# A recurrent-memory attention kernel: the software-DMA ring in SBUF is cut from 16 KB to 4 KB, and three more weight pieces stay resident

## The chip, the core and the metric

The kernel runs on one core of one Trainium2 chip. The metric is the device time of one execution in microseconds (us); lower is better. A core has TensorE (PE; its weight loads are shown as PEld), VectorE (DVE), ScalarE (ACT), GpSimd (POOL) and SyncE (SP), a memory SBUF of 128 partitions, an accumulator memory PSUM of eight banks, and 16 DMA engines that move data between HBM and SBUF. Here SyncE issues the loads of weights, ScalarE and GpSimd issue the other transfers. GpSimd's DMAs are described by software: a piece of each SBUF partition is set aside as a ring in which their descriptors are written.

## The reference

```python
# A: attention with a recurrent memory. x is 2048 x 1024, 32 heads of 128, mem 8 rows, segments of 32 rows
for s in range(64):
    h = concat([mem, x[32 * s:32 * s + 32]])             # 40 rows
    q, k, v = h @ Wq, h @ Wk, h @ Wv                     # 1024 -> 32 heads x 128
    scores = (q @ k.T) * 128 ** -0.5, masked
    o = softmax(scores) @ v
    o = o @ Wo                                           # 4096 -> 1024
    mem = o[:8]                                          # the memory of the next segment
    outs.append(o[8:])
# B: a feed-forward block on the same x, inner width 3584
b = (gelu(x @ w_gate) * (x @ w_up)) @ w_down
g = sigmoid((x * gate_w).sum(-1))
return g * a + (1 - g) * b
```

Each step needs the memory that the step before has made, so the 64 steps run one after the other, and each uses all four weights, 8 MB apiece in bf16.

## The kernel before, in words

The kernel has a prologue (it transposes x, works out the gate, fills the weight slots), a scan of 64 steps, a stage that multiplies the late rows of all segments with Wo (L868), and the feed-forward block with the final mix (from L909 on).

**Pieces and slots.** Each weight is cut into 16 pieces of 128 x 2048 bf16, 512 KB, which is 4 KB of each partition: eight pieces `i` for each half `u` of the heads, 64 pieces `(m, u, i)` with `m` one of k, q, v, o. SBUF holds 50 slots `sl` of that size. A piece is either resident in a slot of its own, or it is one of a pair that shares a slot: `(m, 0, i)` and `(m, 1, i)`, which are loaded in turn. The table `PAIRS` says which `i` are paired, for each weight:

```python
PAIRS = {"k": (1, 3, 5), "q": (0, 2, 5), "v": (0, 2, 4, 6), "o": (0, 2, 4, 6)}
def seq(m, r):
    p = [i for i in range(8) if i in PAIRS[m]]
    f = [i for i in range(8) if i not in p]
    return p + f if r == 0 else f + p
ORDER = (("k", 0), ("q", 0), ("v", 0), ("k", 1), ("q", 1), ("o", 0), ("v", 1), ("o", 1))
```

A step walks through `ORDER` (`r` is the first or second pass over that weight; which half of the heads that is alternates from step to step). In the first pass the paired pieces come first, in the second they come last. As soon as the last use of a paired piece in a step has run on PE (`spent`), the other half is asked for into the same slot (`fetch`, L351, on SyncE's queue); the piece that stays from the second pass is the one that the next step's first pass starts with. So each pair is loaded once per step, 14 loads or 7.3 MB.

**A step on the engines.** `proj` runs the pieces: four matmuls per piece for k, q, v (L662, into the banks X and Y) and eight for o (L674). After each of k, q, v ScalarE copies the bank to `tok` or `vA` (`evac`, L561), PE transposes it (`trans`, L578) and VectorE writes kT or qT. `scores` (L597 to L622) is the score matmul and the softmax, which ends in VectorE's tA and tB; `attend` (L632, L637) multiplies them with vA and vB. Both run twice per step: the scores after the first v and the attention within the second q pass (piece 5), then the scores again after the first o pass and the attention at the start of the second o pass. The step ends in the second o pass, the copy `a_bf`, the transposes at L836 and VectorE's write of the memory rows into hT (L839).

**Work between.** Rows of a segment that don't depend on the memory are projected ahead, four segments at a time: `fill` puts matmuls (L689) into the gaps, `fill_evac` and `fill_put` bring the result through the staging areas kS, qS, oS to the HBM scratch qk_scr and v_scr. From there `load_qk` (L442), `load_v` (L446) and `load_h` (L433) bring in what a step needs. All of these, the store of the result (`store`, L846) and of the late rows (L817) are issued by GpSimd. oS lies on vA's memory, so the copy into vA waits until the stores from oS have landed.

**The end of the scan.** In the last step SyncE's queue gets, after the pieces, the o pieces that the stage L868 needs and that have no slot of their own (`load_xo`, L555), the late rows `oR` (L550), and the first feed-forward weights (L513, L520).

All engines run what the code records in the order of recording; waits are put in from the memory ranges and banks that instructions touch. The sequence on each queue is thus that of the code.

Of the kernel before, what the change touches and what calls it, by code (L numbers as in the profile page):

```python
# [195 lines left out]
def bass_gated_mix__memory_aug_recurrent_mem_tr__geglu_ffn__prompt_kernel(  # L196
# [34 lines left out]
    with ExitStack() as es:  # L231
# [18 lines left out]
        PB = [es.enter_context(nc.psum_tensor(f"pb{i}", [128, 512], FP32)) for i in range(8)]  # L250
        PBV = [p[:, :].bitcast(BF16) for p in PB]

        base = (nc.sbuf_base + 63) // 64 * 64
        top = nc.sbuf_usable_end
        cur = [base]

        def al(name, shape, dt=BF16, at=None):
            if at is None:
                cur[0] = (cur[0] + 63) // 64 * 64
                t = _T(nc, name, shape, dt, cur[0])  # L260
                cur[0] += t.nb
                return t
            return _T(nc, name, shape, dt, at)
# [25 lines left out]
        PIECE = 4096  # L289
        cur[0] = (cur[0] + 63) // 64 * 64  # L290
        res0 = cur[0]
        NSLOT = (top - cur[0]) // PIECE


        PAIRS = {"k": (1, 3, 5), "q": (0, 2, 5), "v": (0, 2, 4, 6), "o": (0, 2, 4, 6)}

        def seq(m, r):
            p = [i for i in range(8) if i in PAIRS[m]]
            f = [i for i in range(8) if i not in p]
            return p + f if r == 0 else f + p  # L300
# [3 lines left out]
        def at_step(p, s):  # L304
            m, r, i = walk[p]
            return (m, r ^ (s % 2), i)

        hosts = []
        for m in "kqvo":
            for i in range(8):  # L310
                if i in PAIRS[m]:
                    hosts.append([(m, 0, i), (m, 1, i)])
                else:
                    hosts += [[(m, 0, i)], [(m, 1, i)]]
        assert len(hosts) <= NSLOT, (len(hosts), NSLOT)
        slots = [al(f"sl{n}", [128, 2048]) for n in range(len(hosts))]
        home = {p: n for n, h in enumerate(hosts) for p in h}
        paired = lambda p: len(hosts[home[p]]) > 1
        uses = [[] for _ in hosts]
        for s_ in range(NSEG):  # L320
            for p in range(64):
                k = at_step(p, s_)
# [49 lines left out]
        for g in range(4):  # L372
            q = slice(32 * g, 32 * g + 32)
# [169 lines left out]
        oR = [al(f"oR{b}", [128, RB, 32], at=tail - (b + 1) * SB * 512) for b in range(NBK)]  # L543
        lost = [("o", 1, i) for i in PAIRS["o"]]
        assert NSEG % 2 == 0
# [185 lines left out]
        for s in range(NSEG):  # L731
            last = s == NSEG - 1
            at = {}
# [258 lines left out]
```

## Time and profile before

| what | value |
|---|---|
| median of 3 runs | 2507.78 us (2507.7, 2507.78, 2512.19) |
| span of the profiled execution | 2512.9 us, 0.7 us above the slowest of the three runs; no other time of that execution is listed |
| busy of the span | PE 84%, DVE 36%, ACT 23%, POOL 23% |
| DMA | 642.77 MB, mean 256 GB/s |
| weight pieces loaded (sl) | 946: Wv 268, Wo 268, Wk 205, Wq 205 |

In lines of the profile the first words are line, engine, operation, tile written and tiles read, with buffer numbers left out. Behind a group's "x" stand the count, then busy us, mean ns, and the idle time before it with what ended it. "SPq" is SyncE's queue of DMA issues. A wait `A <- B: total, times, longest` says that A sat idle until B ended.

### The profile page before, as it was taken

What the parts mean: (1) busy time and instruction counts of PE and PEld (TensorE: products, weight loads), DVE (VectorE), ACT (ScalarE), POOL (GpSimd) and SP (SyncE); (2) the same over time, 40 slices, a digit from 0 to 9 for tenths busy, and PEclk for the clock granted to TensorE, in tenths of its full rate; (3) what the DMA queues carried; (4) which work ended last, traced back from release to release, by engine and by line L of the source; (5) the groups of instructions that cost most, each with busy time, mean ns of one, the idle gap of its engine ahead of it and who ended that gap; (6) DMA issues with size and microseconds to landing.
All of it is one profiled execution on the core that took longest, in us unless ns stands there. A gap on an engine that the chain in (4) does not pass through costs nothing.

```text
span 2512.9 us, 76509 instructions
## 1 busy us (share of the span) xinstructions
PE 2119.3 (84%) x34822; PEld 1062.0 (42%) x34822; DVE 899.3 (36%) x2119; ACT 572.5 (23%) x1175; POOL 587.1 (23%) x1139
## 2 busy tenths in 40 slices
PE   2588888888888888888888888787779999999998
PEld 1244444444444444444444444344445444444443
DVE  3233333333333333333333333333313526354452
ACT  1122222222222222222222222222202303122130
POOL 5223323322332333323333332332200000000000
PEclk9799999999999999999999999999989999999999
DMA  9877887888788788788788788788794070612506
GB/s 359 323 267 280 300 308 281 290 296 296 281 302 309 275 304 317 271 298 317 280 304 305 282 304 310 280 306 313 274 351 175 19 262 5 217 68 91 194 1 218
DMA packets 251859, 642.77 MB, mean 256 GB/s; under 512 B 30344, under 2 KB 43528, under 8 KB 251536
## 3 DMA queue, kind: packets, MB, share of 16 engines
q1 hardware_dynamic: 218128, 584.14, 64.4%
q0 software_dynamic: 23040, 38.87, 5.1%
q10 hardware_dynamic: 10368, 14.88, 1.7%
q8 instruction: 273, 4.47, 0.7%
q14 instruction: 50, 0.41, 0.0%
HBM read 606.29 MB, written 31.39 MB: 254 GB/s over the span
## 4 chain that ended last, share of the span: by engine, by line
PE 44%; DMA 42%; DVE 5%; issue 3%; ACT 3%; POOL 2%; SPq 0%; ACTq 0%; POOLq 0%
DMA sl<-in_A_Wq_dram 17%; DMA sl<-in_A_Wo_dram 14%; PE pb L909 13%; PE pb L674 7%; PE pb L662 7%; PE pb L946 6%; PE pb L689 4%; DMA vB<-v_scr 3%; DMA qk_scr<-oS 3%; PE pb L868 2%; PE pb L578 2%; DMA wd<-in_B_w_down_dram 2%; DMA xr_scr<-xr 1%; ACT tok L561 1%; POOL gp L428 1%
## 5 line engine op out<-in xcount | busy, mean ns | idle before, releaser
L662 PE MATMUL pb<-sl,hT 128*32 128x512 bf16 x12288 | 794.3, 386 | 76.6 <-DMA sl<-in_A_Wq_dram 35.1
L662 PEld LDWEIGHTS pb<-sl,hT 128*32 128x32 bf16 x12288 | 322.2, 97 | 394.5 <-DMA sl<-in_A_Wq_dram 52.3
L674 PE MATMUL pb<-sl,oT 128*32 128x256 bf16 x8192 | 307.1, 292 | 51.1 <-DMA sl<-in_A_Wo_dram 43.6
L561 ACT ACTIVATE tok<-pb 128x512 bf16<-128x512 f32 x320 | 191.3, 598 | 370.3 <-PE pb L662 316.4
L674 PEld LDWEIGHTS pb<-sl,oT 128*32 128x32 bf16 x8192 | 210.8, 103 | 132.8 <-DMA sl<-in_A_Wo_dram 61.9
L689 PE MATMUL pb<-sl,hR 128*32 128x512 bf16 x3072 | 226.8, 393 | 7.4 <-issue 4.0
L909 PE MATMUL pb<-xT,wg 128*128 128x512 bf16 x896 | 211.8, 379 | 8.4 <-DVE GT L925 8.4
L909 PE MATMUL pb<-xT,wu 128*128 128x512 bf16 x896 | 211.7, 379 | 0.0
L646 POOL COPY oRc<-oT 128x128 bf16<-128x128 bf16 x128 | 96.4, 753 | 456.8 <-DVE oT L564 456.8
L946 PE MATMUL pb<-wd,GT 128*128 128x512 bf16 x896 | 195.7, 379 | 3.3 <-DMA wd<-in_B_w_down_dram 3.1
L632 PE MATMUL pb<-tA,vA 32*128 32x40 bf16 x2048 | 36.7, 179 | 143.3 <-DVE tB L622 92.3
L564 DVE COPY qT<-pb 128x512 bf16<-128x512 bf16 x128 | 54.4, 425 | 253.7 <-PE pb L578 240.4
L561 ACT ACTIVATE vA<-pb 128x512 bf16<-128x512 f32 x128 | 76.4, 597 | 279.2 <-DMA v_scr<-oS 106.5
L917 ACT ACTIVATE s<-pb 128x512 f32<-128x512 f32 x112 | 66.8, 596 | 319.2 <-PE pb L909 299.8
L909 PEld LDWEIGHTS pb<-xT,wg 128*128 128x128 bf16 x896 | 86.9, 98 | 116.4 <-DVE GT L925 12.8
L564 DVE COPY kT<-pb 128x512 bf16<-128x512 bf16 x128 | 54.4, 425 | 224.9 <-POOL kT L723 107.9
L946 PEld LDWEIGHTS pb<-wd,GT 128*128 128x128 bf16 x896 | 86.8, 98 | 111.5 <-DMA wd<-in_B_w_down_dram 8.8
L909 PEld LDWEIGHTS pb<-xT,wu 128*128 128x128 bf16 x896 | 87.7, 98 | 105.7
L918 DVE SCALAR_TENSOR_TENSOR tp<-s,pb 128x512 f32<-128x512 f32 x112 | 77.0, 687 | 131.9 <-ACT s L917 131.8
L607 DVE TENSOR_REDUCE st<-pb 128x8 f32<-128x320 f32 x128 | 63.0, 492 | 170.2 <-PE pb L602 170.2
L609 ACT ACTIVATE E<-pb 128x320 bf16<-128x320 f32 x128 | 55.7, 435 | 257.8 <-DVE pb L608 257.5
L561 ACT ACTIVATE oT<-pb 128x160 bf16<-128x160 f32 x256 | 63.8, 302 | 219.5 <-PE pb L637 219.5
(79 smaller groups left out, 1954.7 us busy)
## 6 DMA issues: line engine op xcount, KB each, us to landing
sl<-in_A_Wv_dram SPq DMA_DIRECT2D x268, 512.0 KB, 11.6
sl<-in_A_Wo_dram SPq DMA_DIRECT2D x268, 512.0 KB, 7.3
sl<-in_A_Wk_dram SPq DMA_DIRECT2D x205, 512.0 KB, 5.9
sl<-in_A_Wq_dram SPq DMA_DIRECT2D x205, 512.0 KB, 9.4
wd<-in_B_w_down_dram SPq DMA_DIRECT2D x56, 1024.0 KB, 5.7
qkr<-qk_scr POOLq DMA_DIRECT2D x128, 64.0 KB, 5.8
wg<-in_B_w_gate_dram SPq DMA_DIRECT2D x3, 1792.0 KB, 16.1
wu<-in_B_w_up_dram SPq DMA_DIRECT2D x3, 1792.0 KB, 13.7
```

What stands on the lines that cost most here:

```text
L561: op("act", lambda e: e.activation(o, i, ACTF.Copy), rd=rd, wr=wr)
L564: op("dve", lambda e: e.tensor_copy(o, i), rd=rd, wr=wr)
L607: op("dve", lambda e: e.tensor_reduce(nm, sS, AX.X, ALU.max, negate=True), rd=[BK(SS)], wr=[st8.r(0, 8)])
L609: op("act", lambda e: e.activation(E8[:, :, :].rearrange("p a c -> p (a c)"), PB[SS][:, 0:320], ACTF.Exp, scale=scale), rd=[BK(SS)], wr=[E ...
L646: op("pool", lambda e: e.tensor_copy(oRc[:, :, 16 * u:16 * u + 16].rearrange("p c x -> p x c"), oT[:, :, :, 32:40].rearrange("p g j c -> p ...
L662: ins = e.matmul(PB[bk][32 * g:32 * g + 32, :], lhsT=h[:, i, :], rhs=w[:, g * 512:(g + 1) * 512], start=(p % 8 == 0), stop=(p % 8 == 7))
L674: ins = e.matmul(PB[XO][32 * g:32 * g + 32, 0:256], lhsT=oT[:, gp_, 2 * jj + hh, 0:32], rhs=w[:, c:c + 256], start=(r == 0 and p % 8 == 0 ...
L689: ins = e.matmul(PB[b][32 * g:32 * g + 32, :], lhsT=h[:, k[2], :], rhs=w[:, g * 512:(g + 1) * 512], start=(n == 0), stop=(n == 7))
L909: ins = e.matmul(PB[bk][:, 0:FB], lhsT=w[:, kc, cc:cc + 128], rhs=xT[:, :, :, kc, :].rearrange("p t i c -> p (t i) c"), start=(kc == 0), s ...
L917: op("act", lambda e, hg=hg: e.activation(s1[:, :], hg, ACTF.Square, scale=SQ), rd=[BK(bg)], wr=[s1.r()])
L918: op("dve", lambda e, hg=hg, t=t: e.scalar_tensor_tensor(out=t[:, :], in0=s1[:, :], scalar=1.0, in1=hg, op0=ALU.add, op1=ALU.mult), rd=[BK ...
L946: ins = e.matmul(PB[bank[2 * k + hf]][:, :], lhsT=GT[:, j, tb * 128:(tb + 1) * 128], rhs=w[:, jj, hf * 512:(hf + 1) * 512], start=(j == 0) ...
```

## The change

The ring of descriptors takes 4 KB of each partition instead of 16 KB. The 12 KB behind it are three more slots: the first three of the list lie there (`NLOW`), the others follow where they lay before, so that there are 53. `PAIRS` loses q's 5 and o's 4 and 6, which thereby have slots of their own in both halves. The number of pieces loaded per step falls from 14 to 11 (k 3, q 2, v 4, o 2). What is computed stays the same.

```diff
+        RING = 4096
+        hole = nc.dynamic_dma_scratch_size
+        nc.dynamic_dma_scratch_size = RING
+        for mls in nc.m.functions[0].allocations:
+            if mls.name.startswith("DynamicDMAScratchLoc"):
+                mls.tensor_shape = [128, RING]
+                mls.memorylocations[0].dims = [128, RING]
...
-        NSLOT = (top - cur[0]) // PIECE
-        PAIRS = {"k": (1, 3, 5), "q": (0, 2, 5), "v": (0, 2, 4, 6), "o": (0, 2, 4, 6)}
+        NLOW = (hole - RING) // PIECE
+        NSLOT = NLOW + (top - cur[0]) // PIECE
+        PAIRS = {"k": (1, 3, 5), "q": (0, 2), "v": (0, 2, 4, 6), "o": (0, 2)}
...
-        slots = [al(f"sl{n}", [128, 2048]) for n in range(len(hosts))]
+        slots = [al(f"sl{n}", [128, 2048], at=RING + n * PIECE if n < NLOW else None) for n in range(len(hosts))]
```

Lines of the kernel behind the new ones count nine more (L351 becomes L360). On SyncE's queue, the loads of one step from the first q piece to the last o piece stood like this (the slot's number is the first one in its name):

```order
L351 DMA sl13_85<-in_A_Wq_dram 128x2048
L351 DMA sl16_88<-in_A_Wq_dram 128x2048
L351 DMA sl21_93<-in_A_Wq_dram 128x2048
L351 DMA sl26_98<-in_A_Wv_dram 128x2048
L351 DMA sl29_101<-in_A_Wv_dram 128x2048
L351 DMA sl32_104<-in_A_Wv_dram 128x2048
L351 DMA sl35_107<-in_A_Wv_dram 128x2048
L351 DMA sl38_110<-in_A_Wo_dram 128x2x1024
L351 DMA sl41_113<-in_A_Wo_dram 128x2x1024
L351 DMA sl44_116<-in_A_Wo_dram 128x2x1024
L351 DMA sl47_119<-in_A_Wo_dram 128x2x1024
```

and now stand like this:

```order
L360 DMA sl13_85<-in_A_Wq_dram 128x2048
L360 DMA sl16_88<-in_A_Wq_dram 128x2048
L360 DMA sl27_99<-in_A_Wv_dram 128x2048
L360 DMA sl30_102<-in_A_Wv_dram 128x2048
L360 DMA sl33_105<-in_A_Wv_dram 128x2048
L360 DMA sl36_108<-in_A_Wv_dram 128x2048
L360 DMA sl39_111<-in_A_Wo_dram 128x2x1024
L360 DMA sl42_114<-in_A_Wo_dram 128x2x1024
```

One q load and two o loads are gone; each v load stands one place nearer to the front. On PE, the second o pass of that step, with the transposes of a fill (L713) in it, was this:

```order
L674 MATMUL pb2<-sl39_111,oT_60 32x256 x8
L674 MATMUL pb2<-sl42_114,oT_60 32x256 x8
L674 MATMUL pb2<-sl45_117,oT_60 32x256 x8
L674 MATMUL pb2<-sl48_120,oT_60 32x256 x8
L674 MATMUL pb2<-sl38_110,oT_60 32x256 x8
L713 MATMUL pb3<-ident_49,tok_61 128x128 x4
L674 MATMUL pb2<-sl41_113,oT_60 32x256 x8
L674 MATMUL pb2<-sl44_116,oT_60 32x256 x8
L674 MATMUL pb2<-sl47_119,oT_60 32x256 x8
```

and is now this:

```order
L683 MATMUL pb2<-sl40_112,oT_60 32x256 x8
L683 MATMUL pb2<-sl43_115,oT_60 32x256 x8
L683 MATMUL pb2<-sl45_117,oT_60 32x256 x8
L683 MATMUL pb2<-sl47_119,oT_60 32x256 x8
L683 MATMUL pb2<-sl49_121,oT_60 32x256 x8
L722 MATMUL pb3<-ident_49,tok_61 128x128 x4
L683 MATMUL pb2<-sl51_123,oT_60 32x256 x8
L683 MATMUL pb2<-sl39_111,oT_60 32x256 x8
L683 MATMUL pb2<-sl42_114,oT_60 32x256 x8
```

The count of matmuls is the same. The pieces that come from the stream (sl38, sl41, sl44, sl47 before, sl39 and sl42 now) stand at the end of the pass, two of them now in its last two places.

## The prediction

> **What bounds the kernel now.** I read the page's head first, then the busy time by stage, then who TensorE (PE) waits for in the long middle stage, then single steps in order of time. The head, the stages (columns: window, its length, busy time with instruction counts of PE, PEld, DVE, ACT, POOL, granted clock, share of the 16 DMA engines, GB/s), and the two transposes that close each step (duration in ns, first and last start):
>
> ```profile
> span 2512.9 us, 76509 instructions
> 0.00:112.00 112.00, 40.25 (x469) 22.11 (x469) 35.48 (x67) 16.54 (x29) 44.89 (x49) 0.90 0.98 374
> 139.00:1817.00 1678.00, 1395.14 (x30560) 719.67 (x30552) 573.25 (x1609) 404.89 (x894) 526.41 (x1061) 0.97 0.83 296
> 1817.00:1850.00 33.00, 21.13 (x442) 11.15 (x442) 8.83 (x25) 5.84 (x13) 6.11 (x13) 0.84 0.98 336
> 1850.00:2512.00 662.00, 641.37 (x2944) 298.44 (x2944) 276.12 (x404) 140.36 (x229) 0.00 (x0) 0.99 0.40 137
> L836 PE MATMUL pb<-ident,a_bf x126: 219/229/314, 138.6 to 1816.7; 128*128 128x128 bf16 x126
> ```
>
> The feed-forward half from 1850 us on is 97% PE (641.37 of 662.00) and loads none of the slots that change; I cost it at nothing. L836 runs at the end of each of 63 steps, first at 138.6 and last at 1816.7 us: the scan between is 62 steps of 27.07 us. There PE is busy 1395.14 us, so it idles 282.9 us, 4.6 us a step, while the DMA engines run at a share of 0.83. Who ends that idle time, first for the matmuls and then for the weight loads ahead of them (total us, times, longest):
>
> ```profile
> PE pb L632 <- DVE tB L622: 90.3, 94, 2.0
> PE pb L674 <- DMA sl<-in_A_Wo_dram: 43.6, 55, 1.8
> PE pb L632 <- DMA vB<-v_scr: 43.3, 22, 4.0
> PE pb L662 <- DMA sl<-in_A_Wq_dram: 34.9, 46, 2.3
> PE pb L662 <- DMA sl<-in_A_Wk_dram: 15.9, 20, 1.6
> PE pb L662 <- ACT vA L561: 12.4, 19, 1.2
> PE pb L662 <- DMA sl<-in_A_Wv_dram: 8.7, 17, 0.9
> PEld pb L674 <- DMA sl<-in_A_Wo_dram: 61.9, 66, 2.1
> PEld pb L662 <- DMA sl<-in_A_Wq_dram: 51.6, 59, 2.6
> ```
>
> Two kinds: the softmax and attention chain (tB, vB, vA), and streamed weights. Of the weights, Wo and Wq cost most, and these are the two that the change streams less of. The reason is the order of the queue. Issues of one step on SyncE (start, duration of the burst, count), and the median time to landing over all steps:
>
> ```profile
> 1011.70 1.54 SPq L351 DMA_DIRECT2D sl<-in_A_Wk_dram  x3
> 1014.21 1.38 SPq L351 DMA_DIRECT2D sl<-in_A_Wq_dram  x3
> 1016.38 2.03 SPq L351 DMA_DIRECT2D sl<-in_A_Wv_dram  x4
> 1026.81 2.78 SPq L351 DMA_DIRECT2D sl<-in_A_Wo_dram  x4
> sl<-in_A_Wv_dram SPq DMA_DIRECT2D x268, 512.0 KB, 11.6
> sl<-in_A_Wo_dram SPq DMA_DIRECT2D x268, 512.0 KB, 7.3
> sl<-in_A_Wk_dram SPq DMA_DIRECT2D x205, 512.0 KB, 5.9
> sl<-in_A_Wq_dram SPq DMA_DIRECT2D x205, 512.0 KB, 9.4
> ```
>
> Ten pieces are issued within 6.7 us and land one behind the other: k after 5.9 us, q after 9.4, v after 11.6. So the step has a transfer queue as long as the work that it hides behind, and PE meets its end twice, at the last q piece and at the last o piece.
>
> **The change part by part.** *Third q piece gone (Wq).* In the step shown, the last q piece is the chain's own link, landing 11.00 us after issue, and PE sits until it:
>
> ```profile
> 1015.11 11.00 DMA sl<-in_A_Wq_dram
> 1023.46 0.40 PE L662 MATMUL pb<-sl,hT 128*32 128x512 bf16 x4
> 1026.15 0.40 PE L662 MATMUL pb<-sl,hT 128*32 128x512 bf16 x4 [2.29 <-DMA sl<-in_A_Wq_dram]
> 1026.38 1.15 PE L674 MATMUL pb<-sl,oT 128*32 128x256 bf16 x32
> ```
>
> With two q pieces the last one used is the second of the queue. One piece at the prologue's saturated 374 GB/s is 524,288 B / 374 = 1.4 us, so it lands 1.4 us sooner and is needed at the same place. The mean stall is 34.9 / 46 = 0.76 us; only stalls like this one of 2.29 keep a rest. *Two of four o pieces gone (Wo).* The last one lands two pieces (2.8 us) sooner, and as v is also one piece ahead, still more; the longest stall on it is 1.8 us. I count the Wo stalls as gone.
>
> How much is a stall worth? The named idle time is too low, because a matmul's modelled end runs past the start of its successor:
>
> ```profile
> 1006.75 0.40 PE L674 MATMUL pb<-sl,oT 128*32 128x256 bf16 x8
> 1007.46 0.40 PE L674 MATMUL pb<-sl,oT 128*32 128x256 bf16 x8 [0.30 <-DMA sl<-in_A_Wo_dram]
> 1008.97 0.40 PE L674 MATMUL pb<-sl,oT 128*32 128x256 bf16 x8 [1.12 <-DMA sl<-in_A_Wo_dram]
> 1009.20 1.04 PE L689 MATMUL pb<-sl,hR 128*32 128x512 bf16 x16
> ```
>
> From 1008.97 to 1009.20 an unstalled piece takes 0.23 us. Three pieces from 1006.75 to 1009.20 took 2.45 where 0.69 would do: 1.76 lost, against 0.30 + 1.12 = 1.42 named, 0.17 more per stall. For 55 + 46 stalls that is 17 on top of 43.6 + 34.9 = 78.5: 96. The weight-load rows, which also see stalls shorter than the modelled tail, give 61.9 + 51.6 = 113.5 in 125 stalls. Lower end 78.5, upper end 113.5. I take **-105**, between 96 and 113.5, the mean of both.
>
> *Clock.* After that q stall PE ran one stretch at half clock:
>
> ```profile
> 1027.20:1030.60 3.40, 3.40 (x83) 1.93 (x77) 0.42 (x1) 0.00 (x0) 0.00 (x0) 0.50 0.95 348
> 1030.60:1078.40 47.80, 38.92 (x859) 19.35 (x845) 16.73 (x47) 11.95 (x26) 16.99 (x34) 1.00 0.81 282
> ```
>
> Such a stretch costs half its 3.4 us, 1.7. The scan's mean clock of 0.97 allows at most 0.03 x 1678 = 50 us of it in all, and other stalls (vB, up to 4.0 us) cause it too; 0 to -50, I take **-8**, five stretches, near the low end since only the longest q stalls are seen to do it. The Trainium skill's page "TensorE: Matmul & The Clock Gate" (Part 1: The HAM clock gate) says that the clock falls to half after an idle window of about 3.4 us and returns after a busy one. The trace agrees on the half and on the length; here an idle of 2.29 us with the attention wait ahead of it was enough.
>
> *Wv (8.7) and Wk (15.9).* v's wait sits between the second scores and the second attention, whose wait for tB follows it: a v piece in time only makes that wait longer, 0 (the bounds are -8.7 and 0). The k pieces stand first in the queue, ahead of anything removed: 0 (bounds -15.9 and, as the step gets shorter around them, +5).
>
> *The attention waits (tB, vB, vA).* Their chains start at the scores or at the step's first stores, after the stalls removed, so they move along: 0. Between 0 and 12 us of a step the SyncE queue stays full as before (k, q, then v), so I expect no quicker vB either.
>
> *The end of the scan.* The last step ends in a DMA-bound tail (share 0.98):
>
> ```profile
> 1832.59 2.63 SPq L351 DMA_DIRECT2D sl<-in_A_Wo_dram  x4
> 1836.58 1.91 SPq L555 DMA_DIRECT2D xo<-in_A_Wo_dram  x4
> 1838.70 12.46 SPq L550 DMA_DIRECT2D oR<-o_scr  x3
> 1851.49 1.07 PE L868 MATMUL pb<-sl,oR 128*128 128x512 bf16 x2 [8.12 <-DMA oR<-o_scr]
> ```
>
> PE waits 8.12 us for oR, behind eight pieces; now four stand there. Four pieces at 336 GB/s are 6.2 us; **-5** (bounds -8.1 and 0). *The start.* Three more slots are filled once, 3 x 1.4 = 4.2 us of a saturated stage (0.98), but PE's first steps there do not wait for the last of them: **+1** (0 to +4.2). *Given back.* Rests of q stalls and steps in which another wait steps in: **+5** (0 to +30). *The ring.* 0, see below.
>
> Sum: -105 - 8 - 5 + 1 + 5 = **-112**. The profiled span of 2512.9 would be 2401; it lies 5.1 us above the median of the runs, 2507.78, and the same cut there gives **2396**, 25.3 us a step (the scan's part of the sum is 107, 1.73 a step).
>
> **The rivals.** *Other waits take over.* The attention rows (90.3 + 43.3 + 12.4 = 146) are larger than the Wq and Wo rows together. If the hT load, the k pieces or vB fall behind once the step is shorter, half of the gain goes: about -50, 2458. For it: vB already stalls PE for up to 4.0 us. Against: everything that vB and k depend on is issued after the step's start, and the removed waits lie later.
>
> *More than the sum.* Fewer bytes also shorten the small transfers (vB 43.3, k 15.9) and most half-clock stretches go: -112 less some 60, about 2335. Against: the queue is just as full while vB is under way.
>
> *The ring fills up* (slower). GpSimd's DMAs take descriptors from the ring, and with a quarter of it the queue could have to wait for old ones. One step's end and start, and two landing times:
>
> ```profile
> 1036.46 0.54 POOL L817 DMA_DIRECT2D o_scr<-oRc  x1 [0.29 <-POOL oRc L646]
> 1037.49 0.77 POOL L719 DMA_DIRECT2D qk_scr<-kS  x1 [0.48 <-DVE kS L716]
> 1038.26 0.74 POOL L846 DMA_DIRECT2D a_scr<-a_bf  x1
> 1040.50 2.18 POOL L700 DMA_DIRECT2D v_scr<-oS  x4 [1.51 <-ACT oS L561]
> 1043.62 0.58 POOL L442 DMA_DIRECT2D qkr<-qk_scr  x1 [0.30 <-POOL qT L723]
> 1044.20 0.55 POOL L446 DMA_DIRECT2D vB<-v_scr  x1
> qkr<-qk_scr POOLq DMA_DIRECT2D x128, 64.0 KB, 5.8
> vB<-v_scr POOLq DMA_DIRECT2D x63, 64.0 KB, 6.3
> ```
>
> Nine DMAs in 8.3 us is the densest place, and a landing takes about 6, so nine are in flight at most. If the ring could not hold them, qkr or vB would be held on GpSimd until an older one lands, and the first attention behind it: one wait of 6.3 a step is 63 x 6.3 = 397, less 112, +285: 2793. It decides from 112 / 63 = 1.8 us a step. Against: no issue here is longer than its kind's usual 0.5 to 0.8 us. Counted from the shapes in the code the nine hold 1,536 contiguous runs (512 each in L719 and the four L700, 128 in each other), 96 for each of 16 DMA engines if they are spread evenly. The Trainium skill's page "DMA: Bandwidth & Descriptors" (Terms; SWDGE vs HWDGE vs iDMA) gives 16 bytes a descriptor in rings that lie in that piece of SBUF; by it I estimate 4096 / 16 = 256 in a partition, above 96, and no run here shows a descriptor.
>
> *Nothing changes*: the pieces that remain stall PE as the removed ones did. That needs the last q and o pieces to land no sooner, which the one-by-one landing speaks against.
>
> **How the numbers follow.** Main case 0.76; other waits take over 0.11; more than the sum 0.07; ring 0.04; nothing 0.02. The main case alone spans 2365 to 2435 (ends of the terms: 78.5 with most of the give-back, 113.5 with half of the clock). To hold 8 in 10 the range takes the nearer half of the two neighbours: 2355 to 2445. Differences within 0.2% (5 us) can't be told from none: faster 0.94, same 0.02, slower 0.04.
>
> **What would show it.** Wo and Wq rows of PE's waits: from 78.5 to under 10. tB, vB and Wk rows within a fifth of now. Scan steps of 25.3 us, DMA share about 0.83 x 11 / 14 x 27.07 / 25.3 = 0.70 plus the small transfers' part. The wait for oR near 3 us. GpSimd's issues still 0.5 to 0.8 us. I am wrong if Wk or vB grow by what Wq and Wo lose, or if GpSimd's DMA issues lengthen.

## The result, and the profile after

The changed kernel takes 2383.73 us (median of 4 runs, 2380.43 to 2387.89); before, in the same comparison, 2508.68. The ratio is 0.9501, 95% interval 0.9485 to 0.9517: 125 us or 5.0% faster, where 2396 was predicted. The profiled execution of the changed kernel took 2384.49 us, its span 2382.6.

The head, the stages and the step's closing transposes, as read before (window, length, busy time of PE, PEld, DVE, ACT, POOL, granted clock, DMA share, GB/s):

```profile
span 2382.6 us, 76316 instructions
135.60:1694.20 1558.60, 1347.56 (x30561) 716.83 (x30560) 572.61 (x1609) 404.09 (x894) 527.62 (x1061) 0.99 0.73 256
1727.00:2382.00 655.00, 635.52 (x2929) 295.62 (x2927) 276.00 (x404) 140.37 (x229) 0.00 (x0) 1.00 0.40 135
L845 PE MATMUL pb<-ident,a_bf x126: 219/229/311, 135.4 to 1693.8; 128*128 128x128 bf16 x126
```

The 62 steps between the first and the last closing transpose took 1558.4 us, 25.14 a step, against 1678.1. Of the span's 130.3 us, 119.7 came out of the scan, 3.2 ahead of it and 7.4 behind it. Who PE waits for in the scan:

```profile
PE pb L641 <- DVE tB L631: 92.7, 92, 2.0
PE pb L641 <- DMA vB<-v_scr: 37.2, 23, 3.9
PE pb L671 <- DMA sl<-in_A_Wk_dram: 21.3, 27, 1.6
PE pb L671 <- ACT vA L570: 18.7, 23, 2.0
PE pb L671 <- DMA sl<-in_A_Wv_dram: 3.6, 7, 0.9
PE pb L671 <- DMA sl<-in_A_Wq_dram: 1.7, 4, 0.5
```

There is no row for Wo any more, and Wq is down from 34.9 to 1.7. The three attention rows (tB, vB, vA) are together what they were, 148.6 against 146.0; within them vA rose from 12.4 to 18.7 and vB fell from 43.3 to 37.2. The stall on Wk rose from 15.9 to 21.3. A burst is the pieces of one weight that a step asks for one right behind the other. The bursts of one step that got shorter, the median landings (last number), and the wait at the end of the scan:

```profile
1015.43 0.88 SPq L360 DMA_DIRECT2D sl<-in_A_Wq_dram  x2
1028.01 1.37 SPq L360 DMA_DIRECT2D sl<-in_A_Wo_dram  x2
sl<-in_A_Wq_dram SPq DMA_DIRECT2D x142, 512.0 KB, 9.1
sl<-in_A_Wv_dram SPq DMA_DIRECT2D x268, 512.0 KB, 10.4
sl<-in_A_Wo_dram SPq DMA_DIRECT2D x142, 512.0 KB, 6.0
1722.07 1.50 PE L877 MATMUL pb<-sl,oR 128*128 128x512 bf16 x3 [3.78 <-DMA oR<-o_scr]
```

### The profile page after: what moved, and what is told of

Read it like the earlier page. It is cut to its first block, busy times and chain, and to the rows that moved or that the text cites. A ratio compares the mean times of both kernels' runs of the same rounds, so it can differ in the third digit from the quotient of the medians.

```text
span 2382.6 us, 76316 instructions
## 1 busy us (share of the span) xinstructions
PE 2071.2 (87%) x34822; PEld 1059.3 (44%) x34822; DVE 898.5 (38%) x2119; ACT 571.7 (24%) x1175; POOL 588.2 (25%) x1139
## 4 chain that ended last, share of the span: by engine, by line
PE 48%; DMA 25%; DVE 12%; issue 6%; ACT 5%; POOL 3%; ACTq 0%; SPq 0%; POOLq 0%
PE pb L918 14%; PE pb L683 10%; PE pb L955 6%; DMA vB<-v_scr 6%; DMA v_scr<-oS 5%; DMA qk_scr<-oS 5%; PE pb L671 5%; PE pb L698 4%; DMA sl<-in_A_Wq_dram 3%; PE pb L877 2%; DMA a_scr<-a_bf 2%; DMA wd<-in_B_w_down_dram 2%; DVE st L620 2%; PE pb L587 2%; POOL v_scr L709 2%
## 5 line engine op out<-in xcount | busy, mean ns | idle before, releaser
L671 PE MATMUL pb<-sl,hT 128*32 128x512 bf16 x12288 | 780.5, 384 | 52.5 <-DMA sl<-in_A_Wk_dram 21.3
L671 PEld LDWEIGHTS pb<-sl,hT 128*32 128x32 bf16 x12288 | 316.6, 96 | 350.8 <-DMA sl<-in_A_Wk_dram 38.6
L683 PE MATMUL pb<-sl,oT 128*32 128x256 bf16 x8192 | 277.4, 282 | 2.6 <-ACT oT L570 2.1
L641 PEld LDWEIGHTS pb<-tA,vA 32*128 32x128 bf16 x2048 | 25.0, 92 | 199.0 <-DVE tB L631 97.3
## 6 DMA issues: line engine op xcount, KB each, us to landing
wg<-in_B_w_gate_dram SPq DMA_DIRECT2D x3, 1792.0 KB, 15.9
```

What stands on the lines that cost most here:

```text
L641: e.matmul(PB[bo[g]][:, j * LQ:(j + 1) * LQ], lhsT=vA[r, j, :], rhs=tA[r, 2 * j:2 * j + 2, :].rearrange("p a c -> p (a c)")[:, 0:LQ], star ...
L671: ins = e.matmul(PB[bk][32 * g:32 * g + 32, :], lhsT=h[:, i, :], rhs=w[:, g * 512:(g + 1) * 512], start=(p % 8 == 0), stop=(p % 8 == 7))
L683: ins = e.matmul(PB[XO][32 * g:32 * g + 32, 0:256], lhsT=oT[:, gp_, 2 * jj + hh, 0:32], rhs=w[:, c:c + 256], start=(r == 0 and p % 8 == 0 ...
```

## The experiments

All kernels below are edits of the changed kernel, and each ratio is against the kernel before, run on the same chip in the same comparison.

**1. The ring alone.**

```diff
-        PAIRS = {"k": (1, 3, 5), "q": (0, 2), "v": (0, 2, 4, 6), "o": (0, 2)}
+        PAIRS = {"k": (1, 3, 5), "q": (0, 2, 5), "v": (0, 2, 4, 6), "o": (0, 2, 4, 6)}
```

> The ring has 4 KB and the first three slots lie in the freed space, but the pairs are those of before: 14 pieces streamed per step. Theory (the gain is that of the shorter weight queue; ring and place cost and bring nothing): 2508 us, within 0.3%, Wq and Wo rows of PE's waits together near 78, GpSimd's issues 0.54 to 0.81 us. Rival (the small ring or the new place brings part of the gain, or costs some that the fewer loads hide): at least 15 us off 2508 on either side.

Measured: 2509.9 us, ratio 1.0009 (0.9993 to 1.0026). The stalls on Wo and Wq are those of before:

```profile
PE pb L683 <- DMA sl<-in_A_Wo_dram: 42.0, 54, 1.3
PE pb L671 <- DMA sl<-in_A_Wq_dram: 31.3, 45, 1.7
PE pb L641 <- DMA vB<-v_scr: 35.3, 20, 4.0
PE pb L671 <- DMA sl<-in_A_Wk_dram: 18.3, 26, 1.4
PE pb L671 <- ACT vA L570: 16.0, 24, 1.9
```

So a ring of a quarter of the size, and weights where the ring was, bring and cost nothing that can be measured; the interval leaves some 4 us on the slower side and 2 on the faster. All of the gain is that of the three pieces no longer streamed. The last three rows are worth keeping in mind: with the stream of before, they stand 8.0 below, 2.4 above and 3.6 above what they were, so differences of that size between two profiled executions can't be put down to the pieces. The same goes for the record of the granted clock: 92 us at half clock in the scan here, 109 in the kernel before.

**2 and 3. The q piece alone, the o pieces alone.**

```diff
+        PAIRS = {"k": (1, 3, 5), "q": (0, 2), "v": (0, 2, 4, 6), "o": (0, 2, 4, 6)}      # 2
+        PAIRS = {"k": (1, 3, 5), "q": (0, 2, 5), "v": (0, 2, 4, 6), "o": (0, 2)}         # 3
```

> Small ring, only the third q piece made resident: 13 streamed (k 3, q 2, v 4, o 4). Queue theory (pieces land one behind the other, 1.4 us each, so what is behind a removed piece lands sooner too): Wq row 34.9 to under 5, Wo row from 43.6 to some 20, half-clock stretches mostly gone: about 2415 us. Rival (each piece only cures the stall that names it): Wq row under 5, Wo row at 43 or more, -43 of stalls and -25 of clock: about 2440.

> Small ring, only o's 4 and 6 made resident: 12 streamed (k 3, q 3, v 4, o 2). Both theories: Wo row 43.6 to under 3, wait for oR at the end 8 to about 4, Wq row stays near 35 since q stands ahead of o: about 2445 us. If the half-clock stretches came from the o stalls rather than from q's, about 2425. Queue theory: the savings of this one and of the q piece alone add up to more than the 125 us of both together; rival: to 125 or less.

Measured: q alone 2450.95 us, ratio 0.9759 (0.9728 to 0.9791); o alone 2446.81, ratio 0.9753 (0.9729 to 0.9776). The o row with q's piece gone, and the q row with o's pieces gone:

```profile
PE pb L683 <- DMA sl<-in_A_Wo_dram: 38.3, 44, 1.3
PE pb L671 <- DMA sl<-in_A_Wq_dram: 30.3, 47, 1.5
```

57 and 61 us, together 118, against 125 for both: additive within the intervals. The queue theory had Wo fall to 20 when a piece ahead of it is gone; it fell to 38.3. Here the theory's number failed, and its rival was near (2451 against 2440); which part of the theory failed, experiment 4 shows. The time at half clock fell with q's piece (71 us in the scan, against 92 to 109) and not with o's pieces (112).

**4. The same three slots given to k.**

```diff
+        PAIRS = {"k": (), "q": (0, 2, 5), "v": (0, 2, 4, 6), "o": (0, 2, 4, 6)}
```

> Small ring, the three new slots given to k's 1, 3, 5: also 11 streamed, but q 3, v 4, o 4, none of them q's or o's removed. Queue theory (k stood at the head, so all the rest lands 4 us sooner): Wk row 0, Wq under 10, Wo under 20, and the first stores of a step meet an empty queue, so vB and vA fall too: about 2350 us, below the changed kernel's 2384. Rival (each piece only cures its own stall): Wk's 15.9 and little more: about 2488.

Measured: 2414.41 us, ratio 0.9632 (0.9602 to 0.9661), between the two. Its largest waits that changed, and o's landing:

```profile
PE pb L641 <- DMA vB<-v_scr: 53.7, 32, 3.5
PE pb L683 <- DMA sl<-in_A_Wo_dram: 27.6, 42, 1.2
sl<-in_A_Wo_dram SPq DMA_DIRECT2D x268, 512.0 KB, 6.7
```

No row for Wk, Wq or Wv is left among its larger ones: q, directly behind k, did gain from the shorter queue. o gained less than the queue theory says: 27.6, where under 20 was expected. Worked out from the landing events of 52 steps (mean us from the step's start), the bursts show why:

| kernel | last v lands | o: first issue | o: landings | last o needed |
|---|---|---|---|---|
| before (o of 4) | 19.80 | 15.33 | 21.34, 22.72, 24.12, 25.57 | 25.06 |
| q piece alone (o of 4) | 18.35 | 14.61 | 19.97, 21.62, 23.06, 24.53 | 24.29 |
| k instead (o of 4) | 17.44 | 14.16 | 19.16, 20.86, 22.33, 23.84 | 23.71 |
| changed (o of 2) | 18.31 | 14.53 | 19.85, 21.36 | 23.72 |

("needed" is the start of PE's last o piece less its mean wait.) In every row the first o piece lands 1.5 to 1.7 us after the last v piece, and each further one 1.4 to 1.7 later: o does land behind v, one piece behind the other, as the queue theory says. But a piece that is gone ahead of o also shortens the step ahead of o's issue. The last v lands 1.45 us sooner with the q piece alone and 2.36 sooner with k instead; o's first issue comes 0.72 and 1.17 sooner, so that only half is left for o. From its own issue, o's first piece lands after 6.0 us before, 5.4 and 5.0 in these two.

The length of o's own burst is the other part. A burst of four takes 9.7 to 10.2 us from first issue to last landing, and the work that covers it (first o pass to the last o piece) 9.6 to 9.7. A burst with nothing ahead of it, k's at a step's start or q's in this kernel, has its first landing 4.4 to 4.7 us after its issue. With that, four o pieces would take some 9 us and just fit (an estimate, with 1.45 for each further piece). By these figures both made the stall: a burst that nearly fills the work above it, and before the change some 1.3 us of waiting behind v. Two o pieces fit with 2.4 us to spare.

**5. A ring of 1 KB.** `RING = 1024` in place of 4096.

> As the changed kernel, but with a ring of 1 KB in place of 4 KB (slots of the same number and contents, 3 KB lower). Theory of the ring as a limit that the change stays clear of: now the nine DMAs at a step's end don't fit, GpSimd's issues (0.54 to 0.81 us) lengthen or start later, vB and qkr come later; over 2384 by some 2 to 6 us a step, 2500 to 2760. Rival (the ring is no limit at any such size): 2384 within 0.4%, issues unchanged.

Measured: 2615.01 us, ratio 1.0418 (1.0391 to 1.0444): 231 us over the changed kernel, 3.7 a step. GpSimd's two largest waits of the new kind, and what PE waits for most:

```profile
POOL qk_scr L728 <- issue: 142.8, 29, 7.1
POOL v_scr L709 <- issue: 96.5, 30, 5.7
PE pb L587 <- DVE kT L573: 160.4, 59, 7.6
```

GpSimd stands for up to 7.1 us ahead of a store from oS, though the data is there. The issue itself keeps its 0.54 to 0.82 us; the wait stands between two instructions. One of these waits, and the store ahead of it:

```profile
1033.36 0.74 POOL L855 DMA_DIRECT2D a_scr<-a_bf  x1 [0.90 <-ACT a_bf L570]
1037.89 0.80 POOL L728 DMA_DIRECT2D qk_scr<-oS  x1 [3.78 <-issue]
```

This `a_scr` store lands at 1037.52 by its landing event, 0.37 us before GpSimd goes on. It is so for all 59 of these waits: each ends 0.30 to 0.37 us after the step's `a_scr` store has landed, though the profile shows nothing that GpSimd waits for there ("issue" says just that). Behind the waits come the copies into kT and with them PE's transposes. So the ring that fills up is real, and it is a wait for room that an older DMA frees. 30 of the waits stand among the nine DMAs that the prediction counted (`v_scr`), 29 in other steps (`qk_scr`). In both it is a store from oS that waits, not qkr or vB as the prediction had it, and PE loses the time at its transposes, while its wait for vB falls to 5.9 us. Of the 223 us by which the scan is longer than the changed kernel's, 153 are idle time of PE; PE's busy time for the same matmuls accounts for the other 70, with 275 us at half clock in place of 44. With 4 KB, and with 3 KB in the last experiments, the rows of waits for these two stores show no such thing worth 0.3 us.

**6. No weight streamed at all** (`spent` fetches nothing; a shared slot keeps the weights of one half of the heads, and both halves use them).

> As the changed kernel, but a shared slot is loaded once and never again (both halves of the heads then use the same weights in those pieces): no weight is streamed in the scan. Theory (what weights still cost after the change is k's stall and a little v, with their clock): Wk and Wv rows 0, vB, vA and tB rows within 20% of now: about 2340 us. Rival (the weight loads also slow the small transfers on which vB and vA wait): these rows, 37 and 19, fall to under 15 together and the time to about 2295.

Measured: 2270.32 us, ratio 0.9043 (0.9020 to 0.9065). The theory failed, and its rival holds, by 25 us more than it said (2295):

```profile
PE pb L641 <- DVE tB L631: 124.8, 126, 2.0
vB<-v_scr POOLq DMA_DIRECT2D x63, 64.0 KB, 2.1
v_scr<-oS POOLq DMA_DIRECT2D x124, 32.0 KB, 1.8
```

vB lands in 2.1 us in place of 6.3, the store from oS in 1.8 in place of 5.6, and the rows of vB and vA are gone. So two thirds of what these two small transfers take in the changed kernel come from the weight loads beside them.

**7 and 8. Other splits of 11 pieces.** k's stall of 21.3 is the largest weight stall left; both give k one slot.

```diff
+        PAIRS = {"k": (1, 3), "q": (0, 2, 5), "v": (0, 2, 4, 6), "o": (0, 2)}            # 7
+        PAIRS = {"k": (1, 3), "q": (0, 2), "v": (0, 2, 4, 6), "o": (0, 2, 4)}            # 8
```

> Small ring, also 11 streamed, split k 2, q 3, v 4, o 2. Burst theory (the last piece of a burst lands 4.6 us plus 1.45 per further piece after the first issue, and later only if the burst ahead has not landed): k of two lands at 7.3 us of a step, 2 before it is needed; q of three behind it at 13, 0.8 before; o as in the changed kernel. Wk, Wq, Wo rows all under 6: about 2358 us, below 2384. Rival (own stall only: q's third piece stalls as it did, k's stall goes): Wq near 30 and 2395 or more.

> Small ring, also 11 streamed, split k 2, q 2, v 4, o 3. Burst theory: o of three lands 14.5 + 4.6 + 2.9 = 22.0 us into a step, needed at 23.5, and k and q are clear by 2 us: Wk, Wq, Wo rows all under 6, about 2358 us, equal to the split k 2, q 3, o 2 within 0.4%. Rival (the o stall goes with the bytes per step, about evenly with each piece removed): Wo row near 20 and 2375 to 2385.

Measured: 2410.72 us, ratio 0.9601 (0.9565 to 0.9637), and 2392.8, ratio 0.9524 (0.9486 to 0.9563). The weight stalls did go as the burst theory says: Wk, Wq and Wo are each under 3 in both. The time did not follow; neither beats 2383.7. In 7 and in 8, the copy vA stands in their place:

```profile
PE pb L671 <- ACT vA L570: 33.2, 31, 2.2
PE pb L671 <- ACT vA L570: 35.9, 33, 2.5
```

18.7 before, 33 to 36 now: right behind the k pieces PE needs a bank that the copy into vA has yet to empty, and that copy waits for the store from oS. 15 and 17 of k's 21 us went there. The clock took more than the rest: 89 and 92 us at half clock in the scan, against 44 in the changed kernel, and PE's busy time for the same matmuls up by 15 and 11 us. Number 8 can't be told from the changed kernel by its interval; number 7 is slower.

**9 to 12. The small transfers, taken out of the way.** Number 9 loads vB for the next step right behind the second attention; 10 gives the stores their own kilobyte (with a ring of 3 KB); 11 does both; 12 does both with the split of 8.

```diff
-                on("k", 0, 5, lambda: load_v(s))
+            on("o", 1, 0, lambda: load_v(s + 1) if not last else None)      # behind attend(ub): 9, 11, 12
-        RING = 4096
+        RING = 3072                                                         # 10, 11, 12
...
+        stage = {n: al(n + "S", [128, 512], at=RING if n == "o" else t.off) ...
+        slots = [al(f"sl{n}", [128, 2048], at=RING + 1024 + n * PIECE if n < NLOW else None) ...
```

> The changed kernel with the load of vB moved from the start of a step to the end of the step before, right behind the second attention. Theory (vB is late because its load shares the DMA engines with the weights of the step's start): vB row 37 to under 4, about 2350 us. Rival (the first attention is held as long by the other chain of the step's start: stores from oS, copy vA, softmax, tB): vB's 37 turns into tB and vA, 2375 to 2384 us.

> The changed kernel with a ring of 3 KB, and the fourth KB a staging area of its own for the stores that left from oS on vA's memory, so that the copy into vA needn't wait for their landing. Theory (that landing holds ScalarE's queue and through it the softmax): vA row 19 to under 5 and tB lower, 2355 us. Rival (vB is the later of the two anyway): vA's share goes to vB, 2375 to 2384 us. In both a ring of 3 KB holds the DMAs in flight, with no wait of GpSimd for it.

> Both: vB loaded in the step before, and the staging area of its own (ring 3 KB). If each of the two chains hides the other, this gains more than the two alone together: 2300 to 2320 us, vB and vA rows under 5, half-clock stretches under 30 us. If they are independent, the sum of the two gains.

> Both, and the split k 2, q 2, v 4, o 3 of the 11 streamed pieces. Theory (that split lost its gain on k's stall because the wait for vA stood right behind it): now k's 21 us go for good, 20 to 30 us below the kernel with both alone: about 2285 us. Rival (the split is worse in itself, by o's third piece or by the clock): not below it.

Measured:

| kernel | us | ratio (95%) |
|---|---|---|
| 9, vB early | 2352.65 | 0.9370 (0.9342 to 0.9398) |
| 10, own staging | 2403.09 | 0.9575 (0.9551 to 0.9600) |
| 11, both | 2328.31 | 0.9266 (0.9234 to 0.9298) |
| 12, both and the split | 2311.16 | 0.9204 (0.9180 to 0.9228) |

tB in 9, vB in 10, and the largest wait in 11 and in 12:

```profile
PE pb L641 <- DVE tB L631: 107.9, 110, 1.4
PE pb L641 <- DMA vB<-v_scr: 76.0, 48, 3.3
PE pb L641 <- DVE tB L631: 65.6, 91, 1.4
PE pb L641 <- DVE tB L631: 101.9, 114, 2.0
```

The first attention waits for the later of two chains. Taking away the store's chain alone (10) only showed vB, 37.2 to 76.0, and it ended 19 us slower. Its scan is 10 us longer in the profiled execution, with the same idle time of PE and 68 us at half clock in place of 44; where the rest comes from is not shown, nor was the ring of 3 KB tried without the staging. Taking away vB alone (9) gained 31. Both gained 55, more than -19 and 31 add up to, and half clock fell to 10 us. With vA's wait gone, the split of 8, which had gained nothing by itself, brought another 17. Number 12 beats both kernels: 8.0% below the kernel before and 3.1% below the changed one (0.9204 / 0.9501).

## Why the prediction was right, point by point

The forecast of -112 met -125, and the mechanism was the predicted one: experiments 1 to 3 show that the pieces no longer streamed made the gain, and that the stalls on Wq and Wo went with them. Two terms were mis-sized, in opposite directions, and that the sum came within 13 us is in part luck. (The scan's part of the sum is 108 by its own terms, not 107.)

- *Stalls on Wq and Wo, -105.* The named idle time fell by 76.8 (78.5 to 1.7); with 0.17 us for each of 101 stalls 94. The weight-load rows fell by 109.4 (113.5 to 4.1). Idle and busy time together fell by 119.7, 124.7 without what came back; with the 24 to 33 of the clock below, 92 to 101 are left for the stalls. That is the 96 worked out from the named idle rather than the 113.5 of the weight-load rows, and going halfway was 4 to 13 too much.
- *Clock, -8.* PE's busy time in the scan fell from 1395.5 to 1347.6 for the same matmuls, by 47.9. The stalls' tails are 17 of it, if they are 0.17 each, which leaves 31 for the clock. The record of the granted clock agrees: 109 us at half clock before (28 stretches), 44 now (11), so up to 33 us. With the 92 of experiment 1, whose stream is that of before, it is 24. I took five stretches, and 17 went (15 against experiment 1). The prediction had counted the one stretch that it saw behind a q stall; the mean clock of 0.97 allowed 50, and the far end was the nearer one.
- *Given back, +5.* The idle time fell by 71.8 in all, so 5.0 came back: Wk +5.4, vA +6.3, tB +2.4 against vB -6.1 and Wv -5.1, and small ones. The size is right, but one of the signs that the prediction named, Wk within a fifth of 15.9, did not hold: 21.3 is a third more. Nearly half of that rise stands in experiment 1 too, with all 14 pieces streamed.
- *End of the scan, -5; start, +1.* Measured -7.4 (the wait for oR fell from 8.12 to 3.78) and -3.2. The start's sign was wrong; what of it is the change's was not tried.
- *"As v is also one piece ahead, still more" (Wo).* Right, and small. From first issue to last landing o's burst took 10.2 us before and 6.8 now, 3.4 sooner: 2.8 for two pieces, the rest from v. It was not needed here, since the stall was at most 1.8.
- *Wv and the attention rows, 0.* Right: Wv's 5.1 lie within its bounds, and the attention rows came out 2.6 higher in all.
- *The ring, 0.* Right at 4 KB. At 3 KB no wait for room worth 0.3 us shows either, but that ring was run only beside other changes. The rival's mechanism is shown at 1 KB, at 3.7 us a step where it said 6.3, and ahead of other DMAs than it named.
- *More than the sum* rested on fewer bytes making the small transfers quicker. They did not get quicker (vB 6.3 before and after), as was argued: the queue at a step's start stayed full. Experiment 6 shows that they do when no weight is streamed.

## What to carry to other kernels

Streamed pieces are worth making resident where their burst, from first issue to last landing, takes longer than the work that covers it: take the first issue, the first landing and the spacing from the trace, and compare with the time to the last use. Pieces ahead of it in the queue count too, but a stall cured there brings the burst's own issue forward, and about half of the sooner landing was lost that way here. Before a stall is removed, look at what is late right behind it, as k's gain was lost on vA until the store in front of vA was moved. A region set aside by default can be worth shrinking, if the place where most of it is used at once still fits.

## What the runs showed of the hardware that was not expected

Half clock does not need a whole idle stretch. In the changed kernel PE was busy for 1.51 of 3.5 us, with a matmul burst in between, and the next 3.4 us ran at half clock:

```profile
1021.90:1025.40 3.50, 1.51 (x40) 0.64 (x40) 1.93 (x6) 1.42 (x3) 0.00 (x0) 0.99 1.03 393
1025.40:1028.80 3.40, 3.40 (x56) 1.85 (x48) 0.98 (x3) 1.09 (x3) 1.88 (x4) 0.51 0.89 351
```

In the kernel before and in the changed one, the stretches at half clock in the scan all start whole multiples of 3.41 us from each other. In the changed kernel PE was busy for at most 1.60 us in each of the 11 windows of that grid ahead of a half-clock stretch; of the 432 windows at full clock that full clock followed, three have so little, and none under 1.48.

So where the idle time lies counts as well as how much there is. Over the scan PE stood idle for 207.6, 213.4 and 211.9 us in kernels 7, 8 and 10 (length less busy time of the same windows), and 211.0 in the changed kernel: the same within 4 us. Its busy time, for the same matmuls, was 1362.5, 1359.0 and 1357.1 against 1347.6; by that they lost. And a GpSimd DMA that finds no room showed as a wait ahead of the instruction, in all 59 cases of experiment 5, and not in its duration.
